# Padded query copies moved from GpSimd to VectorE, and strided scores that read queries with a step of four

## The chip, the cores and the metric

The kernel runs on one core of a Trainium2 chip. The core has five engines that run side by side, each through its own list of instructions in order: TensorE (PE; its weight loads, PEld, overlap its products), VectorE (DVE), ScalarE (ACT), GpSimd (POOL) and SyncE (SP). POOL and SP also issue DMAs, which then run on 16 DMA engines. An instruction that needs another engine's result waits for a semaphore, and everything behind it in the same list waits with it. The metric is the device time of one execution in microseconds (us), lower is better. Before the change it is 326.83 us, the median of three runs between 326.56 and 326.98.

## What is computed

Attention over 8 batches, 8 heads, 576 positions and 64 values per head, and behind it a bilinear feed-forward layer. The first four heads see a local window of 32 positions, the last four see every 32nd position up to their own:

```python
scores = scale * np.matmul(q, k.transpose(0, 1, 3, 2))
mask_local = (rel >= 0) & (rel < stride)                       # heads 0 to 3, stride = 32
mask_strided = (rel >= 0) & (pos[None, :] % stride == pos[:, None] % stride)   # heads 4 to 7
attn = softmax(np.where(mask, scores, -1e9))
x = np.matmul(attn, v)                # as [4608 tokens, 512]
out = (x @ w_a) * (x @ w_b) @ w_out   # 512 -> 1536 -> 512
```

## The kernel before

**Order.** The order on every engine is written out by hand. The feed-forward layer is cut into 9 tiles of 512 tokens, and each tile into 16 slots: 12 slots `f` (`ffn_ab`: four products with `w_a`, four with `w_b`, line 612, a ScalarE copy, line 633, and a VectorE product `pf`, line 636), then 4 slots of the output product (`ffn_ys`, lines 816 and 843). The attention of a batch is put between these slots. `STEPS` and `LATER` (lines 570 to 577) say at which slot position each step of a batch is taken: a whole number is the end of a slot, `.5` the middle of it (for 22.5 the middle of slot 23). For batches 3 to 7, `LATER` gives positions relative to slot 16 x (batch - 1). Slots 16 to 31 are those of the second tile, from 57.7 us to 94 us in the profile. A second table, `at`, filled by `do(slot, ...)` (lines 1001 to 1044), holds loads, DMA transposes and smaller work for the end of a slot. From slot 14 on, GpSimd first runs a one-element copy `pace` (line 1054) that waits for the slot's last result, so that its DMAs are not issued too early.

**Steps of a batch.** Scores are made in eight units: `S0` to `S3` of the local heads, `S4` to `S7` of the strided heads. `S` makes TensorE's products into the PSUM tile `st` (line 377), ScalarE's exponent into `p` (line 397) and VectorE's mask (line 415). `V0` to `V3` multiply with the values (line 454) into the PSUM tile `o`, of which there is one buffer, and VectorE scales by the reciprocal of the sums (`rc`, line 462, and `xl`, line 480). `V4` to `V7` do this for the strided heads (line 513, then ScalarE's logarithm and exponent, lines 523 and 524, and VectorE's product, line 527).

**Queries.** Two heads share the 128 partitions, 64 each. So that one product serves one head only, queries are kept in padded tiles `qz0` and `qz1` (even and odd batches; `l` for local heads, `s` for strided): for head j of a pair, its own 64 partitions hold queries and the other 64 hold zeros (`zero_qz`, line 123). From batch 2 (`FIRST_D`) on, keys and queries come by DMA: GpSimd casts rows to DRAM (lines 205 and 207), SyncE's queue transposes them (`step_D`, lines 320 and 323) into `kT` and into `qTl` and `qTs`, and `step_Q` copies `qT` into the padded tile: `Q0` and `Q1` the local heads for j = 0 and 1 (line 335, 64 x 1152 values), `Q2` and `Q3` the strided heads (line 333, two copies of 64 x 576 each). These copies are GpSimd's. `qT` has one buffer.

The strided tile before is laid out as [pair, residue r, j, position n], and `Q2` and `Q3` reorder the queries into it: the four residues that a unit needs stand in `qT` at a step of four, since the transposed rows hold two tokens each. A unit's four products then read 144 contiguous columns each (two heads of 72). Strided keys are not reordered: from batch 2 on, line 376 loads them as weights with a step of four.

**Values.** `load_vl` (line 218) and `load_vs` (line 236) load local and strided values straight into `vl0`/`vl1` and `vs0`/`vs1`. Each value row is followed by columns of ones that give the sums; column D is set at the start (lines 106 and 107), and `fill_v` (line 111) fills columns D to 127 of `vs0` in slot 0 and of `vs1` in slot 28.

**Other work named later.** `fast_s` (line 750, VectorE) makes sums of `pf` for the output product; line 176 does the same for weights; `pair_up` (line 269) and lines 224 and 240 are VectorE copies of batch 1; lines 779 to 787 take the output product out of PSUM.

Of the kernel before, what the change touches and what calls it, by code (L numbers as in the profile page):

```python
# [8 lines left out]
BF16 = mybir.dt.bfloat16  # L9
# [5 lines left out]
FIRST_D = 2  # L15
RL = 6
RS = 8
NP = 72
# [13 lines left out]
def kernel(  # L32
# [10 lines left out]
    nc = tc.nc  # L43
    B, H, S, D = q.shape
# [12 lines left out]
    const = ctx.enter_context(tc.tile_pool(name="const", bufs=1))  # L57
# [9 lines left out]
    def open_psum(stack, **bufs):  # L67
        for nm, n in bufs.items():
# [5 lines left out]
    ident = const.tile([128, 128], BF16)  # L74


    qz_pair = [(const.tile([128, 2, 2, S], BF16, name=f"qz{i}l"), const.tile([128, 2, RS, 2, NP], BF16, name=f"qz{i}s"))
               for i in range(2)]
    qz_buf = [[(l[:, :, j], s[:, :, :, j]) for j in range(2)] for l, s in qz_pair]
    qz_flat = [[l.rearrange("p a b c -> p (a b c)"), s.rearrange("p a b c d -> p (a b c d)")] for l, s in qz_pair]  # L80
    qT = (const.tile([128, 2, S], BF16, name="qTl"), const.tile([128, HL * W], BF16, name="qTs"))
    kT_buf = [(const.tile([128, 2, PAD + S], BF16, name=f"kT{i}l"), const.tile([128, 2, RS * GP + 48], BF16, name=f"kT{i}s"))
# [4 lines left out]
    vs_buf = [const.tile([NP, HL, RS, VW], BF16, name=f"vs{i}") for i in range(2)]  # L87
# [20 lines left out]
        nc.vector.memset(vl_buf[i][:PAD, 0, 0:D], 0.0)  # L108

    def fill_v(t):  # L110
        nc.gpsimd.memset(t[:, :, :, D:] if len(t.shape) == 4 else t[:, :, D:], 1.0)

    spare = const.tile([128, 2], BF16, name="spare")

# [198 lines left out]
    def kT_strided(b):  # L313
        return kT_buf[b % 2][1].rearrange("p c n -> p (c n)")
# [11 lines left out]
    def step_Q(b, z, j):  # L326

        r = slice(64 * j, 64 * j + 64)
        src = qT[z][r]
        if z:  # L330
            src = src.rearrange("d (c h p i) -> d c h i p", c=2, h=2, i=4)
            for c in range(2):
                nc.gpsimd.tensor_copy(qz_buf[b % 2][j][1][r, c].rearrange("d (h i) p -> d h i p", h=2), src[:, c])
        else:
            nc.gpsimd.tensor_copy(qz_buf[b % 2][j][0][r], src)

    def step_Tk(b, c):
        T_p(b, c, "k")
# [6 lines left out]
    def unit(u):  # L345

        c, half = u // 2, u % 2
        return (c, half, 128, LW, 3) if c < 2 else (c, half, NP, NP, 4)
# [9 lines left out]
    def S_p(b, u):  # L358
        c, half, M, n, G = unit(u)
        kT = kT_buf[b % 2][c // 2]  # L360

        st = pst.tile([128, 2, 512], F32, tag="st", name="st")
        held[b, "st", u] = st
        if b > 0:
            sv = st.rearrange("p a (i n) -> p (a i) n", n=256)
            for i in range(G):
                k0 = (G * half + i) * (LW if c < 2 else GP)
                if c < 2:
                    rhs = qz_pair[b % 2][0][:, c % 2, :, k0:k0 + n]
                else:  # L370
                    rhs = qz_pair[b % 2][1][:, c % 2, G * half + i]
                if c < 2 or b < FIRST_D:
                    lhs = kT[:, c % 2, k0:k0 + 128]
                else:
                    k0 = W * (u - HL) + i
                    lhs = kT_strided(b)[:, k0:k0 + 509:4]
                nc.tensor.matmul(sv[:, i, :2 * n].rearrange("p (j n) -> p j n", j=2), lhsT=lhs, rhs=rhs, start=True, stop=True)  # L377
            return
        qz = tl[0, c // 2, "q"]
        if b == 0 and c >= 2:  # L380
            for j in range(2):
                r = slice(64 * j, 64 * j + 64)
                nc.tensor.matmul(st[:, j, :W], lhsT=nm_l[r], rhs=nm_r[r].unsqueeze(1).to_broadcast([64, G, n]),
                                 start=True, stop=False)
        for i in range(G):
            k0 = (G * half + i) * (LW if c < 2 else GP)
            for j in range(2):
                d = slice(64 * j, 64 * j + 64)
                nc.tensor.matmul(st[:, j, i * n:(i + 1) * n], lhsT=kT[d, c % 2, k0:k0 + 128],
                                 rhs=qz[d, c % 2, k0:k0 + n], start=c < 2, stop=c < 2 or i == G - 1)  # L390
# [26 lines left out]
    def S_px(b, u):  # L417
        S_p(b, u)
        S_x(b, u)
# [134 lines left out]
    def step_X(b, c):  # L554
        X_p(b, c)
        X_e(b, c)

    PART = {"Tkp": lambda c: T_p(0, c, "k"), "Tke": lambda c: T_e(0, c, "k"), "Tqp": lambda c: T_p(0, c, "q"),
            "Tqe": lambda c: T_e(0, c, "q"), "Sp": lambda u: S_p(0, u), "Sx": lambda u: S_x(0, u),
            "Sm": lambda u: S_m(0, u), "Vp": lambda u: V_p(0, u), "Vr": lambda u: V_r(0, u), "Vn": lambda u: V_n(0, u),  # L560
            "Xp": lambda c: X_p(0, c), "Xe": lambda c: X_e(0, c)}
# [8 lines left out]
    STEPS = {1: {5.5: "Tk2", 6: "Tq2", 7: "S4 Tk3", 7.5: "S5", 8: "Tq3", 8.5: "V4", 9: "S6 V5 Pk0", 9.5: "S7 Pq0",  # L570
# [4 lines left out]
    LATER = {-6: "Q0", -5: "Q1", -1: "S0", 0: "S1", 1: "V0 Q2", 2: "S2", 3: "V1 O0 Q3", 4: "S3 I0", 5: "V2", 6: "S4", 7: "V3 O1", 8: "S5", 9: "V4 I1",  # L575
             10: "S6",
             11: "V5"}
    IN_Y = {2: "S7", 6: "V6", 11: "V7"}
    FN = {"Tk": step_Tk, "Tq": step_Tq, "S": step_S, "V": step_V, "X": step_X, "W": lambda b, n: fast_w(n, slice(0, 3)),
          "s": S_px, "m": S_m, "L": lead_vl, "O": rows_out, "I": rows_in, "Pk": lambda b, c: pair_up("k", c), "Pq": lambda b, c: pair_up("q", c),  # L580
          "Q": lambda b, n: step_Q(b, n // 2, n % 2)}

    def run(b, slot):
# [323 lines left out]
    with tc.manual_schedule(engines={ENG.PE, ENG.SP, ENG.Pool, ENG.DVE, ENG.Activation}):  # L907
# [30 lines left out]
        for nm in ORDER:  # L938
            if nm[0] == "*":
                spin(int(nm[1:]))  # L940
            elif nm == "C0":
                for x, cp, n in ((raw[0], nc.vector.tensor_copy, "k"), (raw[1], nc.scalar.copy, "q")):
                    t = nats[0, n, False][:, 0:2].rearrange("p h r d -> p (h r d)")
# [21 lines left out]
            elif nm[0] == "F":  # L965
                f = int(nm[1])
# [17 lines left out]
        for b in range(1, B):  # L984
            for pos, names in (STEPS.get(b) or {16 * (b - 1) + x: n for x, n in LATER.items()}).items():
                steps.setdefault(pos, []).append((b, names.split()))
# [6 lines left out]
        def do(i, fn, *args):  # L993
            at.setdefault(i, []).append(lambda: fn(*args))

        soon = {}
        for t in FAST_Y[:-1]:
            if t not in FAST_A:
                soon[16 * t + 10] = [lambda t=t: fast_s(t, 2, slice(4, 6))]
            soon[16 * t + 11] = [lambda t=t, n=n: fast_s(t, n, slice(4, 6)) for n in (0, 1)]  # L1000
        do(0, fill_v, vs_buf[0])
        for c in range(4):
            do(0, load_wo, c)
        do(0, load_vl, 1)
        for b in range(FIRST_D, B):
            g0 = 16 * (b - 2)
            if b == FIRST_D:
                do(0, load_qk, b, False)
                do(1, load_qk, b, True)
                do(15, load_vl, b)  # L1010
                for h in range(HL):
                    do((16, 18, 19, 20)[h], load_vs, b, (h,))
            else:
                do(17 if b == FIRST_D + 1 else g0 - 2, load_qk, b, False)
                do(21 if b == FIRST_D + 1 else g0 + 2, load_qk, b, True)
                for h in range(HL):
                    do(g0 + h + 10, load_vs, b, (h,))
                do(g0 + (10 if b == FIRST_D + 1 else 7), load_vl, b)
            gs = {2: (13, 14, 15, 15), 3: (6, 6, 14, 15)}.get(b) or (3, 4, 10, 11)
            for (z, nm), g in zip(((0, "k"), (0, "q"), (1, "k"), (1, "q")), gs):  # L1020
                do(g0 + g, step_D, b, z, nm)
# [10 lines left out]
        do(4, zero_qz, 1, nc.vector, ((1, 0),))  # L1032
        for i, jz in ((14, (0, 0)), (14, (1, 0)), (15, (0, 1)), (15, (1, 1))):
            do(i, zero_qz, 0, nc.gpsimd, (jz,))
        do(28, fill_v, vs_buf[1])
        for n, slot in enumerate((16, 16, 19, 20)):
            do(slot, fast_w, n, slice(3, 6))
        for g in range(FG):
# [49 lines left out]
```

## Time and profile before

| | us |
|---|---|
| median of three runs | 326.83 |
| the profiled execution, its own time | 326.64 |
| its span, first to last instruction | 324.90 |
| TensorE busy | 315.5 (97%) |
| VectorE busy | 234.1 (72%) |
| ScalarE busy | 186.4 (57%) |
| GpSimd busy | 150.1 (46%) |
| GpSimd query copies, line 333 | 24 copies, 9.5 + 8.4 |
| GpSimd query copies, line 335 | 12 copies, 7.3 + 7.3 |
| granted TensorE clock | 0.997 of full |

A row of a timeline gives the start in us from the span's start, the duration in us, the engine, the line, the operation, what it writes and reads, and in brackets how long the engine stood idle before and what ended that. Equal instructions in a row are merged (x4); their time runs from the first start to the last end, and an instruction's end lies after the next one's start, since both TensorE and VectorE overlap them. A row of an instruction view gives minimum, median and maximum of the durations in ns. In the chain that ended last, the profiler goes back from the last instruction to whatever released each one, and sums this by engine.

### The profile page before, as it was taken

The page shows a single profiled execution, that of the slowest core. Times are in us where ns is not written, and L with a number is a line of the kernel's source. Part 1 is how long each engine was busy: PE and PEld are TensorE (multiplying, and loading weights), DVE is VectorE, ACT ScalarE, POOL GpSimd, SP SyncE. Part 2 cuts the span into 40 slices and gives each one's busy share as a digit, 9 for nine tenths or more (in the row PEclk, how much of TensorE's full clock was granted, in tenths as well). Part 3 has the DMA queues.
Part 4 walks back from the last instruction along what each step waited for, and adds up shares of the span by engine and source line. Part 5 has one row for each costly group of instructions (what it writes and reads, how often), then busy time and mean ns, then how long its engine had stood idle before and what let it go on. Part 6 is the DMA issues. An engine that isn't in the chain of part 4 may idle for free.

```text
span 324.9 us, 7111 instructions
## 1 busy us (share of the span) xinstructions
PE 315.5 (97%) x2706; PEld 214.2 (66%) x2734; DVE 234.1 (72%) x489; ACT 186.4 (57%) x331; POOL 150.1 (46%) x240
## 2 busy tenths in 40 slices
PE   8999999998999999999999999999999999999994
PEld 6754555454765578556999995559555866786684
DVE  6765786498956785688667766777699667857862
ACT  6763766454754476447644765467546655535541
POOL 8944922893785356524652565336124003202520
PEclk9999999999999999999999999999999999999998
DMA  8999999999699999999998999999863030004004
GB/s 150 155 204 196 204 187 204 204 126 175 87 132 153 191 129 101 131 207 167 102 104 181 158 107 107 158 182 112 59 101 103 2 113 17 3 2 129 0 3 129
DMA packets 127234, 40.40 MB, mean 124 GB/s; under 512 B 115040, under 2 KB 124320, under 8 KB 127008
## 3 DMA queue, kind: packets, MB, share of 16 engines
q0 software_dynamic: 80400, 19.28, 64.5%
q1 hardware_dynamic: 46656, 20.61, 36.3%
q8 instruction: 21, 0.34, 0.5%
q14 instruction: 13, 0.11, 0.1%
q10 hardware_dynamic: 144, 0.07, 0.1%
HBM read 39.12 MB, written 18.28 MB: 177 GB/s over the span
## 4 chain that ended last, share of the span: by engine, by line
PE 89%; DVE 4%; ACT 2%; issue 2%; DMA 2%; POOL 0%; ACTq 0%; POOLq 0%
PE mm L612 42%; PE mm L816 18%; PE mm L696 5%; PE st L377 4%; PE mm L878 3%; PE ax L689 3%; PE o L454 2%; PE mm L689 2%; PE o L513 2%; DMA shared<-in_q_dram 2%; PE mm L843 2%; PE end L843 1%; DVE p L415 1%; PE misc L156 1%; PE tp L540 1%
## 5 line engine op out<-in xcount | busy, mean ns | idle before, releaser
L612 PE MATMUL mm<-xT,wb_sb 128*128 128x512 bf16 (+1 forms) x381 | 88.0, 352 | 0.4
L612 PE MATMUL mm<-xT,wa_sb 128*128 128x512 bf16 (+1 forms) x367 | 86.6, 351 | 0.6
L633 ACT COPY a_sb<-mm 128x512 f32<-128x512 f32 x84 | 49.2, 585 | 47.1 <-PE mm L612 45.5
L636 DVE TENSOR_TENSOR pf<-a_sb,mm 128x512 bf16<-128x512 f32 x74 | 50.6, 684 | 26.0 <-PE mm L612 18.4
L612 PEld LDWEIGHTS <-wb_sb 128*128 128x128 bf16 x392 | 37.8, 98 | 33.7 <-issue 0.4
L1054 POOL CAST pace<-pf 1x1 f32<-1x1 bf16 x72 | 21.0, 291 | 77.0 <-DVE pf L636 47.8
L612 PEld LDWEIGHTS <-wa_sb 128*128 128x128 bf16 x392 | 34.9, 98 | 20.9
L397 ACT ACTIVATE p<-st 72x576 bf16<-72x576 f32 (+1 forms) x56 | 36.4, 650 | 20.1 <-PE st L377 19.8
L816 PEld LDWEIGHTS <-ps 128*128 128x128 bf16 x336 | 32.5, 98 | 4.6 <-issue 0.5
L527 DVE TENSOR_TENSOR xT<-o,xr 64x576 bf16<-64x576 f32 x24 | 18.0, 751 | 19.8 <-ACT xr L524 19.6
L816 PE MATMUL mm<-wf,ps 128*128 128x256 bf16 x252 | 30.1, 273 | 0.5 <-ACT y_sb L781 0.3
L781 ACT COPY y_sb<-mm 128x512 f32<-128x512 f32 (+1 forms) x32 | 17.9, 559 | 19.3 <-PE mm L816 16.6
L816 PEld LDWEIGHTS <-pf 128*128 128x128 bf16 x252 | 23.6, 98 | 2.7
L696 PE MATMUL mm<-xT,wb_sb 128*128 128x512 bf16 x83 | 25.3, 379 | 0.1
L816 PE MATMUL mm<-wo_sb,pf 128*128 128x256 bf16 x168 | 21.8, 273 | 0.0
L750 DVE TENSOR_TENSOR ps<-pf 128x512 bf16<-128x512 bf16 (+1 forms) x49 | 21.2, 433 | 0.7
L523 ACT ACTIVATE xr<-o 64x576 f32<-64x576 f32 x24 | 15.6, 648 | 9.4 <-PE o L513 9.2
L1054 POOL COPY pace<-y_sb 1x1 f32<-1x1 f32 x17 | 4.1, 241 | 36.0 <-ACT y_sb L887 13.3
L236 POOL DMA_DIRECT2D vs<-in_v_dram x24 | 20.4, 863 | 0.0
L415 DVE TENSOR_TENSOR p<-p,mask_s 72x576 int16<-72x576 int16 x28 | 18.7, 669 | 1.8 <-ACT p L397 1.5
L454 PEld LDWEIGHTS <-p 128*128 128x128 bf16 (+1 forms) x256 | 13.0, 97 | 8.9 <-DVE xl L480 2.1
L415 DVE TENSOR_TENSOR p<-p,mask_l 128x576 int16<-128x576 int16 x32 | 14.7, 458 | 4.3 <-ACT p L397 4.3
(183 smaller groups left out, 546.7 us busy)
## 6 DMA issues: line engine op xcount, KB each, us to landing
out_dram<-y_sb SPq DMA_DIRECT2D x14, 512.0 KB, 4.9
kr<-in_k_dram POOLq DMA_DIRECT2D x12, 288.0 KB, 5.8
qr<-in_q_dram POOLq DMA_DIRECT2D x12, 288.0 KB, 6.9
vl<-in_v_dram POOLq DMA_DIRECT2D x6, 384.0 KB, 9.5
out_dram<-y_sb SPq DMA_DIRECT2D x7, 256.0 KB, 4.1
vs<-in_v_dram POOLq DMA_DIRECT2D x24, 72.0 KB, 5.9
xd<-xl SPq DMA_DIRECT2D x12, 144.0 KB, 4.8
wo_sb<-in_moe_w_out_dram POOLq DMA_DIRECT2D x4, 384.0 KB, 10.4
```

The lines of the kernel that those rows point to most:

```text
L236: nc.gpsimd.dma_start(out=vs_buf[b % 2][:, h, :, 0:D], in_=v[b, HL + h].rearrange("(p r) d -> p r d", r=RS))
L397: nc.scalar.activation(p_flat(p)[:M, :2 * W].rearrange("p (i n) -> p i n", n=2 * n), st[:M].rearrange("p a (i n) -> p (a i) n", n=256)[:, ...
L415: nc.vector.tensor_tensor(pi, pi, mk, op=ALU.bitwise_and)
L454: nc.tensor.matmul(of[:, j, i, :w], lhsT=pt, rhs=vt, start=True, stop=True)
L527: nc.vector.tensor_mul(dst.rearrange("d (p i j) -> d p i j", i=G, j=2), o[:64, :, :W].rearrange("d j (i p) -> d p i j", p=NP), r)
L612: nc.tensor.matmul(ps_[:, c0:c0 + n], lhsT=w[:, kk, 128 * f:128 * (f + 1)], rhs=xT[:, kk, x0:x0 + n], start=(kk == first and c0 == 0), sto ...
L633: nc.scalar.copy(a_sb, ab[0])
L636: nc.vector.tensor_mul(pf[:, f, :].rearrange("p (i a s) -> p a i s", i=2, s=16), halves(a_sb), halves(ab[1]))
L696: nc.tensor.matmul(got[e], lhsT=wb_sb[:, kk, 128 * f:128 * (f + 1)], rhs=xT[:, kk, x0:x0 + TTOK], start=kk == 0, stop=kk == KD - 1)
L750: nc.vector.tensor_tensor(s[:, n], a, b, op=op)
L816: nc.tensor.matmul(bank[b][:, q], lhsT=lhs(g, q), rhs=rhs(g), start=k in "172" and q == 0 and g == 0, stop=g == FG - 1, skip_group_check=True)
L1054: nc.gpsimd.tensor_copy(pace, done)
```

## The change

- `step_Q` copies queries on VectorE instead of GpSimd, one copy for each of Q0 to Q3 (24 copies in all), and without reordering: the strided padded tile is now [j, pair, residue, position], and a copy fills 1152 contiguous values.
- From batch 2 on, the strided scores read their queries from that tile with a step of four: two runs (one for each head of the pair) of 72 columns. For batches 0 and 1 the layout by residue stays.
- The copies stand elsewhere: in batch 2, Q0 and Q1 at the ends of slots 18 and 19 (before: middle of slot 17), Q2 in the middle of slot 23 (before: end of 20), Q3 at the end of 23 (before: 21). In batches 3 to 7 Q0 and Q1 come two slots later, and Q2 and Q3 one slot later.
- The local values of batch 2 are loaded in slot 14 instead of 15. In the same slot they come ahead of the zeroing of `qz0l`.
- `fill_v` writes columns D + 1 to 127 instead of D to 127, and for `vs1` it runs in slot 2 instead of 28.

In the changed kernel the VectorE copy is line 330, and lines behind it have moved by some lines. TensorE's instructions are the same in number and order.

```diff
-    qz_pair = [(const.tile([128, 2, 2, S], BF16, name=f"qz{i}l"), const.tile([128, 2, RS, 2, NP], BF16, name=f"qz{i}s"))
+    qz_pair = [(const.tile([128, 2, 2, S], BF16, name=f"qz{i}l"), const.tile([128, 2, 2, RS, NP], BF16, name=f"qz{i}s"))
...
-        nc.gpsimd.memset(t[:, :, :, D:] if len(t.shape) == 4 else t[:, :, D:], 1.0)
+        nc.gpsimd.memset(t[:, :, :, D + 1:], 1.0)
...
     def step_Q(b, z, j):

         r = slice(64 * j, 64 * j + 64)
-        src = qT[z][r]
-        if z:
-            src = src.rearrange("d (c h p i) -> d c h i p", c=2, h=2, i=4)
-            for c in range(2):
-                nc.gpsimd.tensor_copy(qz_buf[b % 2][j][1][r, c].rearrange("d (h i) p -> d h i p", h=2), src[:, c])
-        else:
-            nc.gpsimd.tensor_copy(qz_buf[b % 2][j][0][r], src)
+        dst = qz_buf[b % 2][j][z][r]
+        nc.vector.tensor_copy(dst.rearrange("d c r n -> d (c r n)") if z else dst, qT[z][r])
...
                 if c < 2:
                     rhs = qz_pair[b % 2][0][:, c % 2, :, k0:k0 + n]
-                else:
-                    rhs = qz_pair[b % 2][1][:, c % 2, G * half + i]
+                elif b < FIRST_D:
+                    rhs = qz_pair[b % 2][1][:, :, c % 2, G * half + i]
                 if c < 2 or b < FIRST_D:
                     lhs = kT[:, c % 2, k0:k0 + 128]
                 else:
                     k0 = W * (u - HL) + i
                     lhs = kT_strided(b)[:, k0:k0 + 509:4]
+                    rhs = qz_pair[b % 2][1].rearrange("p j c r n -> p j (c r n)")[:, :, k0:k0 + 4 * NP - 3:4]
...
-             2: {16.5: "Q0 Q1", 20: "S0 Q2", 20.5: "S1", 21: "V0 Q3", 21.5: "S2", 22: "V1", 22.5: "S3 O0", 23: "V2", 23.5: "S4",
+             2: {18: "Q0", 19: "Q1", 20: "S0", 20.5: "S1", 21: "V0", 21.5: "S2", 22: "V1", 22.5: "S3 O0 Q2", 23: "V2 Q3", 23.5: "S4",
...
-    LATER = {-6: "Q0", -5: "Q1", -1: "S0", 0: "S1", 1: "V0 Q2", 2: "S2", 3: "V1 O0 Q3", 4: "S3 I0", 5: "V2", 6: "S4", 7: "V3 O1", 8: "S5", 9: "V4 I1",
+    LATER = {-4: "Q0", -3: "Q1", -1: "S0", 0: "S1", 1: "V0", 2: "S2 Q2", 3: "V1 O0", 4: "S3 I0 Q3", 5: "V2", 6: "S4", 7: "V3 O1", 8: "S5", 9: "V4 I1",
...
-                do(15, load_vl, b)
+                do(14, load_vl, b)
...
-        do(28, fill_v, vs_buf[1])
+        do(2, fill_v, vs_buf[1])
```

More of the change, by code (lines that the diff above doesn't have):

```diff
@@ L74 @@
     ident = const.tile([128, 128], BF16)
-    qz_pair = [(const.tile([128, 2, 2, S], BF16, name=f"qz{i}l"), const.tile([128, 2, RS, 2, NP], BF16, name=f"qz{i}s"))
+    qz_pair = [(const.tile([128, 2, 2, S], BF16, name=f"qz{i}l"), const.tile([128, 2, 2, RS, NP], BF16, name=f"qz{i}s"))
                for i in range(2)]
-    qz_buf = [[(l[:, :, j], s[:, :, :, j]) for j in range(2)] for l, s in qz_pair]
+    qz_buf = [[(l[:, :, j], s[:, j]) for j in range(2)] for l, s in qz_pair]
     qz_flat = [[l.rearrange("p a b c -> p (a b c)"), s.rearrange("p a b c d -> p (a b c d)")] for l, s in qz_pair]
```

## The prediction

> **What bounds the kernel now.** I read the page first (busy time, then the chain that ended last), then the timelines of TensorE, VectorE and GpSimd around the third batch, where that chain leaves TensorE, then the instruction views of the lines that change.
>
> ```profile
> PE 315.5 (97%) x2706; PEld 214.2 (66%) x2734; DVE 234.1 (72%) x489; ACT 186.4 (57%) x331; POOL 150.1 (46%) x240
> PE 89%; DVE 4%; ACT 2%; issue 2%; DMA 2%; POOL 0%; ACTq 0%; POOLq 0%
> ```
>
> TensorE is busy nearly always and carries 89% of the chain, so only time in which it stands still can be won. Work on VectorE and GpSimd counts only where TensorE waits for it. After the first 22 us those places are few: one of 0.4 us at 41 us, before the changed work, and a cluster between 72 and 90 us, while batch 2 is attended to for the first time by this path:
>
> ```profile
> 71.83 0.41 PE L377 MATMUL st<-qz0l,kT0l 128*128 128x192 bf16 x3
> 72.08 1.03 PE L612 MATMUL mm<-xT,wb_sb 128*128 128x512 bf16 x4
> 74.18 0.35 PE L454 MATMUL o<-vl,p 128*128 128x65 bf16 x6 [1.07 <-DVE xl L480]
> 74.37 1.03 PE L612 MATMUL mm<-xT,wa_sb 128*128 128x512 bf16 x4
> 75.24 0.41 PE L377 MATMUL st<-qz0s,kT0s 128*128 128x144 bf16 x4
> 75.49 1.03 PE L612 MATMUL mm<-xT,wb_sb 128*128 128x512 bf16 x4
> 76.56 0.35 PE L454 MATMUL o<-vl,p 128*128 128x65 bf16 x6
> ...
> 84.52 1.91 PE L816 MATMUL mm<-wf,ps 128*128 128x256 bf16 x16
> 86.60 0.61 PE L816 MATMUL mm<-wf,ps 128*128 128x256 bf16 x4 [0.17 <-DVE ps L750]
> 87.38 0.42 PE L513 MATMUL o<-p,vs 72*128 72x72 bf16 x8 [0.17 <-DVE xT L527]
> ```
>
> Start to start, four 128x512 products take 0.87 us (74.37 to 75.24). So the first V2 matmul could have started at 72.08 + 0.87 = 72.95; it started at 74.18: 1.23 lost. V3 could have started at 75.49 + 0.87 = 76.36 and did at 76.56: 0.20. Sixteen 128x256 products take 1.75 (0.109 each), so 86.60 is 0.33 late and 87.38 another 0.34. A last stop of 0.48 before 89.86 waits for ScalarE. What VectorE and GpSimd did meanwhile:
>
> ```profile
> 70.42 2.04 DVE L750 TENSOR_TENSOR ps<-pf 128x512 bf16<-128x512 bf16 x1
> 72.39 0.44 DVE L415 TENSOR_TENSOR p<-p,mask_l 128x576 int16<-128x576 int16 x1
> 72.76 0.67 DVE L636 TENSOR_TENSOR pf<-a_sb,mm 128x512 bf16<-128x512 f32 x1
> 73.36 0.18 DVE L462 RECIPROCAL rc<-o 96x6 f32<-96x6 f32 x1
> 73.57 0.55 DVE L480 TENSOR_TENSOR xl<-o,rc 96x384 bf16<-96x384 f32 x1
> ...
> 83.17 1.52 DVE L415 TENSOR_TENSOR p<-p,mask_s 72x576 int16<-72x576 int16 x1
> ```
>
> ```profile
> 70.67 1.50 POOL L333 COPY qz0s<-qTs 64x576 bf16<-64x576 bf16 x2
> ...
> 83.24 1.14 POOL L335 COPY qz1l<-qTl 64x1152 bf16<-64x1152 bf16 x1
> ```
>
> The same line-750 operation takes 0.42 us elsewhere (median 0.416) and the line-415 one 0.454: each was stretched, by 1.62 and 1.06 us, while a GpSimd query copy ran. Batches 3 to 7 show the same stretch (1.52 us at 117.46, 151.13, 185.00, 218.71), but TensorE does not wait there, since VectorE has slack.
>
> **The change part by part.**
>
> *GpSimd copies removed.* 24 copies of line 333 and 12 of line 335, 32.5 us of GpSimd time, off the path themselves. With them the stretches go. At V2: line 750 ends at 70.75, the mask of S2 follows ScalarE's exponent (70.12 + 0.65) at 70.81, pf at 71.30, rc 71.91, xl 72.12 to 72.67. V2 is then ready before its turn at 72.95, so 1.23 goes; V3's 0.20 goes too, and at 86 us 0.67. The ScalarE stop of 0.48 stays: V6, logarithm, exponent and copy follow each other whatever VectorE does. Together 2.10 us.
>
> *VectorE copies added.* 24 copies of 64x1152. No such row exists; the nearest are
>
> ```profile
> L224 DVE COPY vl<-vl x2: 350/351/352, 50.1 to 52.6; 32x704 bf16<-32x704 bf16 x1, 32x768 bf16<-32x768 bf16 x1
> L269 DVE COPY tq<-shared x2: 345/694/1042, 40.4 to 42.0; 96x768 bf16<-96x768 bf16 x2
> L269 DVE COPY shared<-shared x1: 346/346/346, 43.7 to 43.7; 96x768 bf16<-96x768 bf16 x1
> ```
>
> and line 240's 72x512 at 0.27 us. From 512 to 768 elements 0.075 us are added, so 1152 elements take about 0.35 + 0.11 = 0.46 (0.35 at least; 0.35 x 1.5 = 0.53 if the whole scales). The 1.04 of line 269 stood beside two DMA issues on GpSimd: up to 0.70 more where that happens. VectorE gets 11 us of copies and loses 8.2 us of stretch (1.62, five of 1.06, and 0.53, 0.38, 0.19, 0.17), so its 72% stays about as it is. In batches 3 to 7 the copies lie in slots where TensorE had no wait and no wait is shortened to nothing: Q1 comes two slots (3.9 us) before S0, Q3 two before S4. Their DMAs have landed too: qTs of batch 3, the latest, landed at 99.95 and its copy stands behind a mask that started at 101.04. I cost these at nothing; if a landing came 1.5 us later, that mask's followers would queue behind the copy.
>
> *Where the copies stand in batch 2.* Here is the new wait. VectorE works in order, and Q3 is put behind V2's scaling, in slot 23; S4 is TensorE's next but one stage. By the durations above: xl of V1 leaves VectorE at 72.60, line 750 until 72.97 (S3's exponent, 72.28 + 0.65, ends then), the mask until 73.34, Q2 until 73.71, pf until 74.31, rc and xl of V2 until 75.00, Q3 ends at 75.46. Without the old stop TensorE reaches S4 at 72.95 + 0.19 + 0.87 = 74.01 and waits until about 75.50: 1.49 new. S4 then starts 0.26 later than now (75.24), though V2 came 1.23 earlier. Bounds: 0.4 if Q3 needed only V2's own end (73.3), rc, xl and itself; 2.2 if a DMA issue holds it 0.7 longer.
> Q1 stands behind pf at 64.91 + 0.60 and ends at about 65.97, before S0 at 66.37; GpSimd, relieved of its copies, now issues line 207's loads (1.3 to 2.2 us) about then. Bounds 0 and 0.35; I take 0.15.
>
> *Strided reads of the queries.* 6 batches x 4 units x 4 = 96 matmuls now read two runs of 72 columns at a step of four. No matmul here reads its moving side so. The nearest rows are the weight loads of the same matmuls, which already use that step:
>
> ```profile
> L377 PEld LDWEIGHTS <-kT0s x48: 111/113/116, 75.0 to 220.5; 128*128 128x128 bf16 x48
> L377 PE MATMUL st<-qz0s,kT0s x48: 226/226/226, 75.2 to 220.5; 128*128 128x144 bf16 x48
> L377 PEld LDWEIGHTS <-kT0l x36: 95/98/98, 66.2 to 205.1; 128*128 128x128 bf16 x36
> ```
>
> The step costs a load 15 ns over 128 columns, and the products still follow each other at 62 ns (four in 0.25 us). Lower bound 0. By the same ns per column, 17 ns x 96 = 1.7 us. Upper bound, the read at half speed: 144 columns in 60 ns become 120, 96 x 60 = 5.8 us. I take 0: step two costs line 816's loads nothing (98 ns), so slowdown sets in near here, and a load takes its columns faster than a matmul (line 513's pairs of load and 72 columns follow at 32 ns), so a matmul stresses the memory less.
> The Trainium skill, "SBUF — State Buffer", "Door 1: The DMA port swizzle", says that SBUF reads run at full bandwidth while at least two accesses fall into each 16-byte line. A step of four bf16 makes exactly two, so by it the sum has 0 here. The 15 ns of the loads do not agree with it for weights; no run here shows it for the moving side.
>
> *The rest.* The local values of batch 2 are issued at about 55.3 instead of 58.95; they landed at 67.30, before V0 at 68.62: nothing waited, 0. The earlier transfer shares the DMA engines with the transposes of kT0l and qTl, which landed at 60.16 and 61.59; Q0 needs the latter at 63.8, S0 the former at 66.37: cover 2 us. The fill of vs1 (1.82 us) leaves GpSimd at 89.8 and goes to about 42.7 to 44.5, where GpSimd was idle until 55. A VectorE copy of line 269 starts there at 43.67; held to the end of the fill it would end at 44.85, before its reader at 45.35. 0.
>
> **Sum.** The profiled execution took 326.64 (span 324.90 and 1.74 around it), 0.19 below the median 326.83. 326.64 - 2.10 + 1.49 + 0.15 + 0 = 326.18; with the 0.19, a median of 326.4: 0.14% less, which is no change by the 0.2% (0.65 us) that a measurement of this kernel can tell.
>
> **The rivals.**
> 1. *The step of four slows the matmuls* (slower). Place: line 377 of batches 2 to 7. Half speed gives 326.4 + 5.8 = 332.2; the loads' price gives 328.1. For it: the 15 ns. Against: the 62 ns spacing already hides strided loads. It decides from 1.1 / 96 = 11 ns a matmul on.
> 2. *The S4 wait is short* (faster). If VectorE runs a little ahead of my chain and S4 waits 0.4, the rest of the 2.10 stays: 326.83 - 2.10 + 0.4 = 325.1. For it: the chain sums seven operations, each by its spacing. Against: the in-order place behind V2.
> 3. *VectorE copies and GpSimd block each other*: DMA issues hold Q0 to Q3 0.7 us each in batch 2, and S0, V1 and S4 come late: 326.4 + 1.2 = 327.6. For it: line 269's 1.04. Against: after 71 us GpSimd has only single-element casts to do near Q2 and Q3.
> The skill's same page, "Who interferes with whom", says that a VectorE copy in a two-port mode and a GpSimd instruction lock each other out for the whole instruction. The 1.04 against 0.35 agrees; by that rule rival 3 is what would happen if GpSimd's issues fall on the copies.
>
> **Chances and range.** Forecast 0.43 (own range 325.8 to 327.3; 0.11 of it faster, 0.31 the same, 0.01 slower), rival 2 0.22 (faster), rival 1 0.28 (0.16 at half speed, 0.12 at the lesser price, of which 0.01 stays the same), rival 3 0.07 (0.04 slower, 0.03 the same). Faster 0.33, same 0.35, slower 0.32. The range takes in the S4 wait's lower bound and the half-speed read, since both signs hold much: 325.0 to 332.4.
>
> **What would show it.** Right: line 750 and 415 never over 0.8 us; V2 without a stop near 72.9; a stop of about 1.5 before the first line-377 matmul of S4, released by VectorE's copy (line 330); copies of about 0.46; strided matmuls 62 ns apart, 226 ns each. Wrong: those matmuls longer or further apart (rival 1), no stop before S4 (rival 2), or copies of an us beside DMA issues (rival 3).

## The result, and the profile after

The changed kernel takes 334.88 us, the median of four runs between 334.61 and 338.2. The kernel before, run beside it on the same chip, takes 326.9 (326.56 to 327.41). The ratio is 1.027, with a 95% interval from 1.020 to 1.033: slower by 8 us, where no change was forecast, and outside the range. Ratios and intervals, here and below, leave out executions that took over 1.5% more than the fastest of their kernel, such as two of 331 us of the kernel before. The profiled execution of the changed kernel took 334.61, with a span of 332.3 instead of 324.9.

The busy times of its page:

```profile
PE 321.9 (97%) x2706; PEld 220.2 (66%) x2734; DVE 239.3 (72%) x513; ACT 186.1 (56%) x331; POOL 121.4 (37%) x204
```

GpSimd lost 28.7 us of work and VectorE gained 5.2. The balance that was worked out had 32.5 and 2.8; of VectorE's difference one copy of 2.80 us, shown below, makes 2.3. But TensorE is busy 6.4 us longer with the same 2706 instructions. Its instruction view for the strided scores (line 373 here, 377 before; durations are minimum, median and maximum in ns) says which:

```profile
L373 PE MATMUL st<-qz0s,kT0s x48: 289/309/313, 76.9 to 226.7; 128*128 128x144 bf16 x48
```

Before, each took 226. What counts is the distance from one start to the next. Summed over the 24 units of batches 2 to 7, four products take 0.507 us on average, not 0.250. That is 24 x 0.257 = 6.2 us.

TensorE's timeline around batch 2 shows the rest:

```profile
65.29 1.03 PE L608 MATMUL mm<-xT,wb_sb 128*128 128x512 bf16 x4
67.61 0.41 PE L373 MATMUL st<-qz0l,kT0l 128*128 128x192 bf16 x3 [1.29 <-POOL pace L1050]
...
73.31 1.03 PE L608 MATMUL mm<-xT,wb_sb 128*128 128x512 bf16 x4
74.18 0.35 PE L450 MATMUL o<-vl,p 128*128 128x65 bf16 x6
74.36 1.02 PE L608 MATMUL mm<-xT,wa_sb 128*128 128x512 bf16 x4
76.92 0.68 PE L373 MATMUL st<-qz0s,kT0s 128*128 128x144 bf16 x4 [1.54 <-DVE qz0s L330]
77.43 1.04 PE L608 MATMUL mm<-xT,wb_sb 128*128 128x512 bf16 x4
```

Four 128x512 products take 0.87 us from start to start. V2 could start at 73.31 + 0.87 = 74.18 and does: the stop of 1.23 us is gone. S0 could start at 65.29 + 0.86 = 66.15 and starts at 67.61: a new stop of 1.46. S4 could start at 74.36 + 0.86 = 75.22 and starts at 76.92: a new stop of 1.70. The strided unit itself lasts 76.92 to 77.43, twice its 0.25 of before.

S4 had to wait for Q3, which stands behind V2's scaling on VectorE and ended at 76.78:

```profile
75.75 0.55 DVE L476 TENSOR_TENSOR xl<-o,rc 96x384 bf16<-96x384 f32 x1
76.32 0.46 DVE L330 COPY qz0s<-qTs 64x1152 bf16<-64x1152 bf16 x1
```

VectorE's timeline, and then GpSimd's, say who kept S0 waiting:

```profile
63.57 2.80 DVE L330 COPY qz0l<-qTl 64x1152 bf16<-64x1152 bf16 x1
66.30 0.67 DVE L632 TENSOR_TENSOR pf<-a_sb,mm 128x512 bf16<-128x512 f32 x1
67.00 0.47 DVE L330 COPY qz0l<-qTl 64x1152 bf16<-64x1152 bf16 x1
```

```profile
62.84 1.63 POOL L207 DMA_DIRECT2D kr<-in_k_dram  x1 [0.23 <-issue]
63.95 2.15 POOL L207 DMA_DIRECT2D qr<-in_q_dram  x1
```

Q0's copy started during the first of GpSimd's two DMA issues and ended 0.27 us after the second (66.10). It took 2.80 us. Q1 had to follow it and `pf`, ended at 67.47, and S0 started. The page puts the stop down to GpSimd's `pace`, but what S0 reads came last from VectorE. Of the other 23 copies one took 0.64 us, and the rest took what was estimated:

```profile
L330 DVE COPY qz0s<-qTs x6: 444/450/458, 74.6 to 211.8; 64x1152 bf16<-64x1152 bf16 x6
```

The balance against the span of before: 324.9 - 2.10 (stops of before, all gone) + 6.16 (the step) + 1.46 (S0) + 1.70 (S4) = 332.1, against 332.3 measured. Another 0.57 us lies outside the span (2.31 instead of 1.74). The step does not make it, since `contiguous_read` below has 2.24 there and `step_alone` 1.71; its cause was not tried.

### The profile page after: what moved, and what is told of

It reads as the page before. It is cut to its first block, busy times and chain, and to the rows that moved or that the text cites. A ratio compares the mean times of both kernels' runs of the same rounds, so it can differ in the third digit from the quotient of the medians.

```text
span 332.3 us, 7095 instructions
## 1 busy us (share of the span) xinstructions
PE 321.9 (97%) x2706; PEld 220.2 (66%) x2734; DVE 239.3 (72%) x513; ACT 186.1 (56%) x331; POOL 121.4 (37%) x204
## 4 chain that ended last, share of the span: by engine, by line
PE 89%; POOL 3%; DVE 2%; ACT 2%; issue 2%; ACTq 0%
PE mm L608 39%; PE mm L812 18%; PE st L373 6%; PE mm L692 5%; PE ax L685 3%; PE misc L156 3%; PE o L450 2%; PE mm L874 2%; PE mm L685 2%; PE o L509 2%; PE mm L839 2%; PE end L839 1%; POOL qr L207 1%; PE tp L289 1%; PE tp L280 1%
## 5 line engine op out<-in xcount | busy, mean ns | idle before, releaser
L608 PEld LDWEIGHTS <-wa_sb 128*128 128x128 bf16 x392 | 36.0, 99 | 21.5
L1050 POOL COPY pace<-y_sb 1x1 f32<-1x1 f32 x17 | 4.8, 281 | 44.1 <-DVE y_sb L775 22.9
L746 DVE TENSOR_TENSOR ps<-pf 128x512 bf16<-128x512 bf16 (+1 forms) x49 | 19.6, 400 | 0.8
L411 DVE TENSOR_TENSOR p<-p,mask_s 72x576 int16<-72x576 int16 x28 | 12.6, 451 | 6.3 <-ACT p L393 6.2
```

The source lines that it names most:

```text
L411: nc.vector.tensor_tensor(pi, pi, mk, op=ALU.bitwise_and)
L608: nc.tensor.matmul(ps_[:, c0:c0 + n], lhsT=w[:, kk, 128 * f:128 * (f + 1)], rhs=xT[:, kk, x0:x0 + n], start=(kk == first and c0 == 0), sto ...
L746: nc.vector.tensor_tensor(s[:, n], a, b, op=op)
L1050: nc.gpsimd.tensor_copy(pace, done)
```

## The experiments

Each time stands beside runs of the kernel before made on the same chip. Letters in the expectations: A is that the step of four slows the matmuls; C that GpSimd's DMA issues hold Q0 and so S0, with D as its rival, that the later landing of `qTl` (63.41 instead of 61.59) does it; E that Q3's late place in VectorE's order makes the S4 stop; F to J are explained where they appear.

### The step taken away

```diff
-                    rhs = qz_pair[b % 2][1].rearrange("p j c r n -> p j (c r n)")[:, :, k0:k0 + 4 * NP - 3:4]
+                    q0 = W * (u - HL) + NP * i
+                    rhs = qz_pair[b % 2][1].rearrange("p j c r n -> p j (c r n)")[:, :, q0:q0 + NP]
```

> The changed kernel, but the strided scores of batches 2 to 7 read 72 contiguous columns per head instead of 72 at a step of four. These are the wrong queries, so the strided scores are not the reference's; copies, waits and the number and size of all instructions stay. Theory A (the step of four slows the matmuls): the 96 matmuls follow each other at 62 ns again instead of about 131, which takes 96 x 0.066 = 6.3 us off the 334.9: 328.6. The stops before S0 (1.46) and S4 (1.70) stay. Theory B (the loss is VectorE's: its copies, and waits that follow from them): the time stays at 334 to 335, since nothing on VectorE changes.

Measured: 328.12 us, 1.004 of before (1.0004 to 1.008), span 325.9, 6.4 less than with the step. The products are back at 226 ns and 62 ns apart:

```profile
L374 PE MATMUL st<-qz0s,kT0s x48: 226/226/227, 77.1 to 221.5; 128*128 128x144 bf16 x48
```

The stops before S0 (1.46) and S4 (1.70) are unchanged. So the step alone costs 6.4 us, and the two stops do not come from it. Even so the kernel is not faster than before, since 3.16 of new stops outweigh 2.10 of old ones.

### The step alone

In the kernel before: the plain strided tile, plain copies of 64x1152 on GpSimd at their old places, reads at a step of four.

```diff
-            for c in range(2):
-                nc.gpsimd.tensor_copy(qz_buf[b % 2][j][1][r, c].rearrange("d (h i) p -> d h i p", h=2), src[:, c])
...
+        dst = qz_buf[b % 2][j][z][r]
+        nc.gpsimd.tensor_copy(dst.rearrange("d c r n -> d (c r n)") if z else dst, qT[z][r])
...
+                    rhs = qz_pair[b % 2][1].rearrange("p j c r n -> p j (c r n)")[:, :, k0:k0 + 4 * NP - 3:4]
```

> The kernel before with one part of the change alone: the strided query tile in the plain layout, plain copies of 64x1152 still on GpSimd at their old places, and the strided scores read at a step of four. Theory A (the step costs 66 ns a matmul wherever it is used, 96 x 66 ns = 6.3 us): 326.8 + 6.3 = 333.1 us, with the strided matmuls about 130 ns apart, and the stops of before (1.23 us ahead of V2, 0.67 us near 86 us) still there. Rival A0 (the step is slow only beside the VectorE copies of the change): matmuls 62 ns apart and 326.8 us.

Measured: 332.2 us, 1.016 of before (1.011 to 1.020), span 330.3, products about 130 ns apart. The step costs the same without VectorE's copies; A0 falls. The time is 0.9 under A's: of the 2.1 us of old stops only 0.3 at V2 and 0.1 near 87 us were left in this execution, and a stop of 0.75 ahead of V0, for batch 2's values, was new (324.9 + 6.2 - 2.1 + 1.2 = 330.2).

### Which steps cost what

```diff
+                    st_ = (1, 2, 3, 4, 6, 8)[b - FIRST_D]
+                    q0 = min(k0, HL * W - st_ * (NP - 1) - 1)
+                    rhs = qz_pair[b % 2][1].rearrange("p j c r n -> p j (c r n)")[:, :, q0:q0 + st_ * (NP - 1) + 1:st_]
+                    if u >= 6:
+                        k0 = min(k0, HL * W - 128)
+                        lhs = kT_strided(b)[:, k0:k0 + 128]
```

> The changed kernel, with another step of the query read in each batch: 1, 2, 3, 4, 6 and 8 in batches 2 to 7. Units S4 and S5 load their weights with a step of four as before, S6 and S7 load 128 contiguous columns. The strided scores are not the reference's. Theory A1 (cost follows the 16-byte lines that a read touches): a step of 2 still runs at 62 ns a matmul, 4 at about 131, 8 at about twice that. Theory A2 (anything but contiguous columns is read at half speed): 2 to 8 all at about 120 to 131. Theory A3 (strided weight loads and strided reads get in each other's way): with contiguous weights step 4 falls from 131 to 62 ns. The time, by A1: four batches of six cheaper or about as dear, so 332 to 337.

In the second such kernel only the steps differ, and the weights are strided throughout:

```diff
-                    st_ = (1, 2, 3, 4, 6, 8)[b - FIRST_D]
+                    st_ = (4, 8, 10, 12, 14, 16)[b - FIRST_D]
```

> The changed kernel with the step of the strided query reads at 4, 8, 10, 12, 14 and 16 in batches 2 to 7 (the queries read are the wrong ones, so the strided scores of those batches are wrong). Theory A1 (a read pays by the 16-byte stretches of SBUF that it touches, 1.8 ns each for 144 of them): 4 at 130 ns, and 8 to 16 all at about 257 ns a matmul. Rival A4 (a read pays by the bytes that it spans, 8.9 bytes a ns): 8 at 257, 10 at 322, 12 at 386, 14 at 450, 16 at 514 ns.

The first kernel's instruction view in the stretches of batches 4, 5 and 7 (steps 3, 4 and 8), and the second's of batches 3 and 7 (steps 8 and 16):

```profile
L378 PE MATMUL st<-qz0s,kT0s x16: 256/262/271, 147.0 to 159.1; 128*128 128x144 bf16 x16
...
L378 PE MATMUL st<-qz1s,kT1s x16: 289/308/312, 181.4 to 194.1; 128*128 128x144 bf16 x16
...
L378 PE MATMUL st<-qz1s,kT1s x16: 414/435/437, 252.0 to 266.5; 128*128 128x144 bf16 x16
```

```profile
L375 PE MATMUL st<-qz1s,kT1s x16: 417/436/442, 110.0 to 124.5; 128*128 128x144 bf16 x16
...
L375 PE MATMUL st<-qz1s,kT1s x16: 421/440/445, 257.5 to 272.1; 128*128 128x144 bf16 x16
```

| step | start to start, ns (mean of the last three of a unit) | stretches of 16 bytes that 2 x 72 columns touch | ns per stretch |
|---|---|---|---|
| 1 | 64 | 18 | - |
| 2 | 67 | 36 | 1.87 |
| 3 | 99 | 54 | 1.83 |
| 4 | 131 | 72 | 1.81 |
| 6 | 193 | 108 | 1.79 |
| 8 | 256 to 258 | 144 | 1.78 |
| 10, 12, 14, 16 | 260, 258, 260, 262 | 144 | 1.79 to 1.82 |

The third column is counted from the addresses: bytes spanned over 16, but never more than one for each column. The time follows it at 1.8 ns each, from step 2 on, and stands still from step 8 to 16, where the bytes spanned double. So the account by stretches holds and the one by bytes (A4) falls. In the first kernel half of each batch's units had contiguous weights. At step four they took 500 and 498 ns for four products, the others 505 and 506, so the weight loads add 2 ns a product at most. The total times (339.4 and 345.2 us, one run each) are of no use here, since they mix the steps, and the first kernel's execution also had a stop of 2.4 us near 40 us (see the last section).

### The S0 stop: batch 3's local loads three slots later

```diff
-                do(17 if b == FIRST_D + 1 else g0 - 2, load_qk, b, False)
+                do(20 if b == FIRST_D + 1 else g0 - 2, load_qk, b, False)
```

> The changed kernel, but GpSimd issues the casts of batch 3's local keys and queries in slot 20 instead of 17, behind the copies Q0 and Q1 of batch 2. Theory C (Q0's 2.80 us is time in which GpSimd, issuing these two loads, keeps the VectorE copy from running): Q0 takes 0.46 us, the stop of 1.46 before S0 goes, 334.9 falls to 333.4. Theory D (Q0 waits for its data, since the earlier load of local values delays the transpose of qTl): the stop stays, 334.9.

Measured: 333.81 us, 1.023 of before (1.020 to 1.027), span 330.9, 1.4 less than the changed kernel. Of its VectorE timeline the copies Q0 and Q1:

```profile
63.63 0.44 DVE L330 COPY qz0l<-qTl 64x1152 bf16<-64x1152 bf16 x1
...
65.47 0.46 DVE L330 COPY qz0l<-qTl 64x1152 bf16<-64x1152 bf16 x1
```

Q0 starts as late as in the changed kernel (`qTl` landed at 63.45), yet takes 0.44 us, and S0 has no stop. So the two issues of line 207 made it, and the later landing did not. The S4 stop of 1.70 is still there.

### The S4 stop: Q2 and Q3 one stage earlier

```diff
-... 21.5: "S2", 22: "V1", 22.5: "S3 O0 Q2", 23: "V2 Q3", 23.5: "S4",
+... 21.5: "S2 Q2", 22: "V1", 22.5: "S3 O0 Q3", 23: "V2", 23.5: "S4",
```

> The changed kernel, but in batch 2 Q2 stands in the middle of slot 22 and Q3 in the middle of slot 23, so that Q3 is no longer behind V2's scaling. Theory E (S4 waits for Q3's place in VectorE's order): the stop of 1.70 before S4 shrinks to 0.3 or less, 334.9 falls to about 333.4. Theory F (VectorE simply has too much to do there): the stop moves to V2, V3 or a product behind them, and the time stays within 0.4 us of 334.9.

Measured: 333.32 us, 1.021 of before (1.018 to 1.024), span 330.5. Of the stop before S4 0.20 is left (it starts at 75.14, where 74.08 + 0.87 = 74.95 was the earliest). That is E: the place in VectorE's order made the wait. In this execution `qTl` landed only at 65.27, so Q0 waited 2.0 us for it and S0 had its stop of 1.45 all the same: a late landing can make that stop too, but did not in the changed kernel.

### The three costs out together

Contiguous reads, the later loads and the earlier copies at once (the three diffs above).

> The changed kernel with the three costs taken out together: contiguous reads of 72 queries in the strided scores (the layout is not made for them, so the strided scores of batches 2 to 7 are wrong), batch 3's local loads in slot 20, Q2 and Q3 of batch 2 one stage earlier. Theory H (the time after is the time before, less the 2.1 us of stops won, plus 6.4 for the step, 1.46 for S0 and 1.70 for S4, and nothing else): 326.8 - 2.1 = 324.7 us. Rival H0 (there is a fourth cost, such as the fill of vs1 at 42 us): 325.3 us or more, with a stop of TensorE near 40 us longer than the 0.6 us of before.

Measured: 327.4 us, 1.001 of before (0.999 to 1.003). Neither theory as written. The three costs are gone, but the edits that removed them bring waits. V2 is 0.78 us late. The place of Q2 ahead of V2's scaling is not enough to explain it, since in `earlier_q2q3` Q2 has the same place, takes 0.44 us, and V2 is on time. Here the later loads push GpSimd's line-205 issues next to it, and Q2 takes 1.20:

```profile
71.75 1.20 DVE L330 COPY qz0s<-qTs 64x1152 bf16<-64x1152 bf16 x1
```

```profile
71.81 1.40 POOL L205 DMA_DIRECT2D kr<-in_k_dram  x1
```

So the clash that had held Q0 has moved to Q2. Another 0.50 is lost near 95 us, because `xT`, SyncE's DMA transpose, landed at 95.25 (92.85 before). S4 and V3 lose 0.2 each, the stops between 37 and 42 us come to 1.04 instead of 0.71, and 0.2 is lost ahead of 34 us. Together this takes all of the 2.1 us that the change frees.

### Other ways to free VectorE

The first keeps the layout of before and puts all reordering copies on VectorE, at the change's places but Q2 and Q3 earlier; the smaller edits beside it are in the expectation.

```diff
-                nc.gpsimd.tensor_copy(qz_buf[b % 2][j][1][r, c].rearrange("d (h i) p -> d h i p", h=2), src[:, c])
+                nc.vector.tensor_copy(qz_buf[b % 2][j][1][r, c].rearrange("d (h i) p -> d h i p", h=2), src[:, c])
```

> The kernel before's layout and contiguous reads, but every query copy on VectorE (the strided heads' in two reordering copies a step), Q2 and Q3 of batch 2 one stage earlier than in the change, batch 3's local loads in slot 20, batch 2's local values in slot 15, the fill in slot 2. Theory G (what the change meant to win is there once its three costs, the step, the S0 stop and the S4 stop, are taken out): 326.8 - 2.1 = 324.7 us, up to 325.5 if the reordering copies take 0.75 us each instead of 0.45. Rival G0 (reordering copies are slow on VectorE, over 1 us a pair, and hold the masks of S2 to S4): new stops ahead of V2 to V4 and 326.5 us or more.

Measured: 328.04 us, 1.003 of before (0.9996 to 1.006). In the profiled execution (331.97 us) Q2's pair of reordering copies took 1.56 us and Q3's 0.83, ahead of V2's and V3's scaling, and stops of 1.15 and 0.58 us stood there. The stops are G0's, its cause only in part: a reordering copy of 64x576 takes 0.44 to 0.46 us, as long as a plain one of twice the size, so that a pair takes 0.83. Q2's pair took more because its first copy, at 75.80, ran beside GpSimd's line-205 issues, the first at 75.87, and took 1.20, as in `three_undone`.

The second moves batch 2's Q2 and Q3 to ScalarE; the smaller edits beside it are in the expectation.

```diff
+        cp = nc.scalar.copy if b == FIRST_D and z else nc.gpsimd.tensor_copy
...
-             2: {16.5: "Q0 Q1", 20: "S0 Q2", 20.5: "S1", 21: "V0 Q3", 21.5: "S2", 22: "V1", ...
+             2: {16.5: "Q0 Q1", 20: "S0", 20.5: "S1", 21: "V0 Q2", 21.5: "S2", 22: "V1 Q3", ...
```

> The kernel before (its layout, its contiguous reads) with four edits: the copies Q2 and Q3 of batch 2 on ScalarE behind V0 and V1, the fill of vs1 without its column D and in slot 2, and Q0 and Q1 of batch 3 three slots later on GpSimd. Theory F (the stops of before come from GpSimd's copies beside VectorE's operations, as the prediction had it): VectorE's lines 750 and 415 no longer stretched between 70 and 86 us, the stops of 1.23, 0.20 and 0.67 us gone, and 326.8 - 2.1 = 324.7 us. Rival F0 (TensorE only meets the next wait: ScalarE is now late with an exponent): about 326.8 us, and a stop released by ScalarE between 72 and 78 us.

Measured: 327.0 to 342.5 us in six runs, median 333.16, too far apart to say anything of the time. In the profile (span 327.7) F's first half holds: no operation of lines 751 and 416 is over 0.7 us between 70 and 86 us, V2 has no stop, and no exponent is late. But the fill of `vs1` in slot 2 held a VectorE copy of line 269 for 2.35 us (TensorE 1.72 late), `xT` came 1.89 late, and S4 of batch 3 came 0.77 late.

So the ScalarE copies were tried with nothing else moved:

> The kernel before with one edit: Q2 and Q3 of batch 2 on ScalarE behind V0 and V1 (0.71 us each of four copies). Theory F again, with nothing else moved: the stop of 1.23 us before V2 gone, the 0.67 us near 86 us still there (the copy of batch 3's local queries stays on GpSimd), 326.8 - 1.23 = 325.6 us. Rival F0: a stop for an exponent of ScalarE in its place, 326.8 us.

Measured: 331.81 us, 1.014 of before (1.011 to 1.017). The stop at V2 is gone, and two much larger ones are new. TensorE's timeline of the profiled execution (333.96 us, the longest of six):

```profile
94.15 0.41 PE L378 MATMUL st<-qz1l,kT1l 128*128 128x192 bf16 x3 [2.40 <-POOL qz1l L336]
...
100.33 0.58 PE L613 MATMUL mm<-xT,wa_sb 128*128 128x512 bf16 x1 [4.12 <-DMA xT<-xd]
```

GpSimd, rid of two copies, issued batch 3's strided loads (line 205) at 71.22 instead of 74.50 us, 0.36 behind the DMA transpose of its local keys. The transpose then landed 17.3 us after its issue instead of 6.0, with the queries' transpose, Q0 of batch 3 and SyncE's next transposes behind it. Beside the two stops (2.56 and 4.54 us by the starts) TensorE lost time to its clock: between 94 and 106 us 0.57 of it was granted. The tile view's answer for those keys:

```profile
DMA to landing us min/median/max: 17.3/17.3/17.3
```

With the local heads' copies on VectorE as well, and the local loads in slot 20:

```diff
-            nc.gpsimd.tensor_copy(qz_buf[b % 2][j][0][r], src)
+            nc.vector.tensor_copy(qz_buf[b % 2][j][0][r], src)
...
-             2: {16.5: "Q0 Q1", 20: "S0", ...
+             2: {18: "Q0", 19: "Q1", 20: "S0", ...
...
-    LATER = {-6: "Q0", -5: "Q1", ...
+    LATER = {-4: "Q0", -3: "Q1", ...
...
-                do(17 if b == FIRST_D + 1 else g0 - 2, load_qk, b, False)
+                do(20 if b == FIRST_D + 1 else g0 - 2, load_qk, b, False)
```

> scalar_only, and the local heads' query copies on VectorE where the change has them (0.45 us each), with batch 3's local loads in slot 20 as in later_load. Theory F: the 0.67 us near 86 us go too, 326.8 - 1.23 - 0.67 = 324.9 us. Rival F1 (VectorE's copies and the later loads bring waits of their own): a stop before S0 or after 90 us, 325.6 us or more.

Measured: 326.7 us, 0.998 of before (0.996 to 1.001): no difference shown. F1: stops of 0.59 (S3), 0.78 (V2), 0.33 (V3) and 0.83 (`xT`) took what was won. The first three come from ScalarE: its copies for Q2, which waited for `qTs` to land at 70.12 (68.18 before), and for Q3 stood ahead of the exponents.

Last, `scalar_only` with batch 3's strided loads apart from the transposes:

```diff
-                do(21 if b == FIRST_D + 1 else g0 + 2, load_qk, b, True)
+                do(23 if b == FIRST_D + 1 else g0 + 2, load_qk, b, True)
```

> scalar_only with one edit more: batch 3's loads for the strided heads (line 205 of before) in slot 23 instead of 21. In scalar_only they were issued at 71.22 us, 0.36 us behind the transpose of batch 3's local keys (70.86), which then landed after 17.3 us instead of 6.0, with S0 of batch 3 and the products after it late. Theory J (the nearness of these two transfers does it): the transpose lands within 7 us of its issue again, the stops of 2.6 us before S0 of batch 3 and of 4.5 us behind it are gone, and theory F's gain shows: 326.8 - 1.23 = 325.6 us. Rival J0 (the transpose is slow because of the earlier loads of line 236 or 207): it still takes over 12 us, and about 331 us.

Measured: 324.63 us against 326.23 of the runs of before beside it; the ratio is 0.995 (0.994 to 0.997). The transpose landed 7.3 us after its issue, a little over the 7 expected, and V2 follows its products at once. The tile view's answer for the keys, then TensorE's timeline:

```profile
DMA to landing us min/median/max: 7.3/7.3/7.3
```

```profile
76.84 1.03 PE L613 MATMUL mm<-xT,wb_sb 128*128 128x512 bf16 x4
77.70 0.35 PE L455 MATMUL o<-vl,p 128*128 128x65 bf16 x6
```

The big stops are gone; of the wait for `xT` 0.46 is left in the profiled execution. (That one took 329.86 us, mostly because of a stop near 42 us that the last section tells of.) Two slots for one load turn a kernel that is 1.4% slower into one that is 0.5% faster than before: J. How the nearness slows the transfers no run shows. The kernel beats both others. In its profile the 0.67 us near 86 us is gone too, though the copy blamed for it is still GpSimd's: the copy waited for `qTl` to land at 87.28 and started 0.74 us behind the mask that it had stretched before, and the 0.33 by which it stretched a line-751 operation instead cost TensorE nothing. With it, 1.23 + 0.67 - 0.46 = 1.44 of the 1.6 us won are named.

## Why the prediction was wrong

**The strided reads** are the step that failed. Its term was 0, with an upper bound of 5.8; they cost 6.2 to 6.4. Rival 1 happened, beyond its half-speed price: a read at half speed was put at 120 ns for 144 columns, and the products stand 131 apart (113 for the first of a unit). Two arguments for 0 were wrong. From line 816's loads, free at step two, it was said that slowdown sets in near step four; the runs show it at step three already (99 ns). And that a load takes its columns faster than a matmul was taken to mean that a matmul stresses the memory less. A load may take longer unseen, since the next one overlaps the running product (113 against 98 ns, products still 62 apart); the moving read sets the distance from product to product, and here nothing hid it. A price measured on the hidden side was carried to the side that has no cover.

The Trainium skill, "SBUF — State Buffer", "Door 1: The DMA port swizzle", gives full bandwidth from two accesses in each 16-byte line on. For the moving side the runs do not agree: two accesses (step four) take 131 ns, four (step two) 67, eight (step one) 64.

**The S0 wait** was put at 0.15 with bounds 0 and 0.35, and measured 1.46. The place was named (line 207's issues beside the copies), but the 0.70 of line 269's copy beside two issues was taken for the most that could happen, and it was charged to Q1. Q0 was held, until both issues had ended, and `pf` and Q1 behind it. This is rival 3's mechanism on one copy, at over three times its price. The Trainium skill, "SBUF — State Buffer", "Who interferes with whom", has the lock last for the whole instruction of the other engine. The 2.80 us agrees, but it outlasted two instructions, which overlap in the profile.

**The S4 wait** was right: 1.49 forecast, 1.70 measured, by the chain that was named; `earlier_q2q3` confirms the cause. Rival 2 fell.

**The gain** was right: all stops of lines 750 and 415 (746 and 411 after) are gone, 2.10 us in the balance, and ScalarE's 0.48 stays. In `step_alone`, where the copies stayed on GpSimd, line 746 was still stretched, to 1.80 us, but V2 lost only 0.3: TensorE, after its new stop ahead of V0, came 0.5 us later to it, and VectorE was done 0.4 us earlier.

**The copies** were right: 0.44 to 0.47 us for 22 of 24, 0.46 forecast, and they cost nothing in batches 3 to 7. So was the rest, in this execution: `qTl` landed 1.8 us later, within its cover of 2 (not so in `earlier_q2q3`), and the fill held a line-269 copy to 44.5 us, before its reader.

With the terms as measured the forecast's sum is 326.64 - 2.10 + 1.70 + 1.46 + 6.16 = 333.9, and with the 0.57 outside the span 334.4 of the 334.61 measured.

## What to carry to other kernels

Price a strided operand on the side that sets the pace: count the 16-byte stretches of a partition that a matmul's moving read touches, at about 1.8 ns each here (measured for two runs of 72 bf16 columns only), and keep a reordering copy if that exceeds the time per column. When work is taken off an engine that also issues DMAs, list what it will issue earlier, and look at which copies and which transposes those issues will then meet; `scalar_only` and `scalar_split_loads` differ in this alone, by 1.8%. Moving an issue can move the clash, as `three_undone` shows, where the later loads freed Q0 and held Q2. Where an engine works in order, the place of a new copy can cost more than its length: 0.46 us of copy cost a wait of 1.70 here.

## What the runs showed of the hardware that was not expected

- A moving read of 144 bf16 columns takes 64, 67, 99, 131, 193 and 257 ns at steps 1, 2, 3, 4, 6 and 8, and 258 to 262 at steps 10 to 16.
- Near 40 us executions differ though their instructions up to there are the same, as those of `steps_by_batch` and the changed kernel are. When a 72x512 VectorE copy (line 240) starts just after the first of GpSimd's two line-207 issues (37.7 to 38.0 us), it takes 2.8 to 3.05 us instead of 0.28. TensorE stops for some 2.5 us and then runs for a while with products 120 ns apart instead of 62; between 42 and 48 us 0.72 of its clock was granted. It fell so in the profiled executions of `steps_by_batch`, `vector_reorder` and `scalar_split_loads`, but not in those of the kernel before and the changed kernel. In VectorE's timeline of `vector_reorder`:

```profile
38.22 2.94 DVE L240 COPY vs<-tk 72x512 bf16<-72x512 bf16 x1
```

- The DMA transpose of batch 3's local keys landed after 9.7 us (`earlier_q2q3`), 11.8 (`scalar_q23`) and 17.3 (`scalar_only`) where GpSimd's line-205 loads were issued within 0.4 us of it. With the loads 1.6 us or more behind it, it took 5.0 to 7.3 us. This holds for that transpose only: the next one, of the queries, was issued within 0.4 us of those loads in the changed kernel and in `contiguous_read`, and took 7.9 and 8.1 us.
